# Attention and a sine mixture on one core: angles rounded straight from PSUM, and the exponentials ordered around the sines

## The chip, the cores and the metric

The kernel runs on one core of a Trainium2 chip. The metric is the time of one execution on the device in microseconds; the median of three runs is quoted. Engines are named as the profile names them: PE is TensorE (matrix products, and transposes as products with a unit matrix), DVE is VectorE, ACT is ScalarE, POOL is GpSimd, SP is SyncE, which issues most of the DMA.

## The reference

Two layers follow each other. Attention over 8 batches of 8 heads, 576 positions and head size 64, keeps for each query only the scores within `tau` of that row's largest. The mixture then works on each batch as a 576 x 512 matrix.

```python
scores = scale * q @ k.T                      # per batch and head, 576 x 576
thresh = max(scores, -1, keepdims) - tau
attn = exp(where(scores >= thresh, scores, -1e9) - max)
x = (attn / (sum(attn) + 1e-9)) @ v           # 576 x 512 per batch, heads side by side
theta = x @ w_theta                           # 512 x 512
y = w_tok_r @ (x * cos(theta)) + w_tok_i @ (x * sin(theta))
u = x + y
out = u + maximum(u @ w_ch, 0)
```

## The kernel before

Attention goes over 32 pairs of heads, four to a batch. A pair has 4 units of 128 query rows for each of its two heads, and a ninth step for the last 64 rows of both, so nine steps ("halves"). One half goes through these instructions:

- score: TensorE multiplies q and k into `s_ps`, of which there is one buffer (L278); VectorE copies it out with its sign turned and takes the row minimum as it goes (`sc`, L282).
- softmax: VectorE makes the limit of the row (`nm`, L295), ScalarE the exponentials (`s_sb`, L299), VectorE compares, multiplies and sums in one scalar_tensor_tensor (L300).
- flip: TensorE transposes `s_sb` into `t_ps` (L326, L341), ScalarE copies it out (L331, L333, L344, L348).
- values: twice a pair, 20 matmuls make `o_ps` (L361), and ScalarE copies it to `xT` (L362).
- normalize: once a pair, the reciprocals of the row sums are spread by TensorE (`rb_ps` L377, `rl_ps` L381) and multiplied in by VectorE (L383, L386).

Scores and softmax are issued three halves ahead of the flips. The tiles `t_ps`, `o_ps`, `rb_ps`, `rl_ps`, and `m_ps`, `z_ps`, `y_ps` below share six PSUM buffers, so a matmul that starts a new tile waits until the oldest of the six has been read out.

When the four pairs of a batch are through, the mixture of that batch (`moe`) is woven in between the halves of the next batch. It is a generator that gives TensorE's work out in small groups; `fill()` takes from it as much as falls due. For each of four blocks m of 128 columns it does:

- angle: TensorE makes the angle in two pieces of 288 columns (`m_ps`, L405). Each piece is copied to `th` in units of full turns, by ScalarE for m = 0 and 1 (L444) and by VectorE for m = 2 and 3 (L446). When both pieces are there, VectorE rounds `th` to whole turns by adding and subtracting a large constant, MAGIC (`km`, L453), and subtracts (`th`, L454).
- sines, for two blocks at a time (m = 0 and 1 are the first series, 2 and 3 the second): VectorE makes the absolute value (`z`, L463), ScalarE loads the table of the sine (L467), makes cosine (L471, a sine of a quarter turn less the absolute value) and sine (L472) of both blocks, and loads the table of the exponential again (L476). GpSimd multiplies the four results by x (`z`, L483); in the last batch VectorE does that.
- flips of z: TensorE transposes `z` (L495), ScalarE rounds to a high part (`zh`, L497), VectorE takes the rest (`zl`, L498).
- token: TensorE multiplies with the token weights (`y_ps`, L512), VectorE adds to `xT` (L515). Later follow the products with `w_ch` (L405 again) and L560.

The order within a batch is `a0 a1 s01 a2 a3f0 s23 t0f1 t1f2 t2f3 t3`: a an angle product, s a series of sines, f a flip of z, t a token product. The tiles `th`, `km`, `rb`, `qraw` and `kraw` share four buffers ("t576").

The order of TensorE's instructions is the order in which the code is written (`manual_schedule`). The order on the other engines is made by a scheduler from priorities and a timeline of its own: attention is lifted by `ATTENTION`, the ScalarE instructions of a series by `SINES`. `after(a, b)` asks for a behind b on one engine, without a semaphore. Before the change, nothing says how the exponentials L299 stand to a series, except its lift: one that comes due inside a series takes its own two table loads with it.

Of the kernel before, what the change touches and what calls it, by code (L numbers as in the profile page):

```python
# [12 lines left out]
U32 = mybir.dt.uint32  # L13
AF = mybir.ActivationFunctionType
ALU = mybir.AluOpType
# [24 lines left out]
def tile_attn_moe(  # L40
# [70 lines left out]
    def temp(name, dt=F32):  # L111
        return pool.tile([P, S], dt, tag="t576", name=name, bufs=4)
# [5 lines left out]
        return ins  # L118

    turn = [0]  # L120

    def load_weight(src, n, on_pe=True):

# [168 lines left out]
    def softmax(u, j):  # L292

        nm = u.nm
        nc.vector.tensor_scalar(  # L295
            out=nm[:, 2 + j : 3 + j], in0=nm[:, j : j + 1], scalar1=span, scalar2=None, op0=ALU.add
        )
        e = u.s[:, j]
        nc.scalar.activation(out=e, in_=u.ps[j], func=AF.Exp, bias=nm[:, j : j + 1], scale=-1.0)  # L299
        nc.vector.scalar_tensor_tensor(  # L300
            out=e,
            in0=u.ps[j],
            scalar=nm[:, 2 + j : 3 + j],
            in1=e,
            op0=ALU.is_le,
            op1=ALU.mult,
            accum_out=u.pr.rows[:, 2 * u.i + j : 2 * u.i + j + 1],
        )
# [119 lines left out]
    def moe(b):  # L428
# [7 lines left out]

        def angle(m):
            th = temp("th")
            wm = get_wm(0, m)

            def evict(ps, hs):

                if m < 2:
                    nc.scalar.activation(out=th[:, hs], in_=ps[:, :HS], func=AF.Copy, scale=1.0 / TURN)  # L444
                else:
                    nc.vector.tensor_scalar(  # L446
                        out=th[:, hs], in0=ps[:, :HS], scalar1=1.0 / TURN, scalar2=None, op0=ALU.mult
                    )

            yield from product(wm, xs, evict, m == 0)  # L450

            km = temp("km")
            nc.vector.tensor_scalar(out=km, in0=th, scalar1=MAGIC, scalar2=-MAGIC, op0=ALU.add, op1=ALU.add)  # L453
            nc.vector.tensor_tensor(out=th, in0=th, in1=km, op=ALU.subtract)  # L454
            zs[m, "f"] = th

        def sines(ms):

            todo = []
            for m in ms:  # L460
                th = zs.pop((m, "f"))
                z = pool.tile([P, 2 * S], F32, tag="z", name="z", bufs=3)
                ab = nc.vector.tensor_scalar(  # L463
                    out=z[:, :S].bitcast(U32), in0=th.bitcast(U32), scalar1=0x7FFFFFFF, scalar2=None, op0=ALU.bitwise_and
                )
                todo.append((m, th, z))
            ahead_of = after(nc.scalar.preload_act_table(AF.Sin), ab)  # L467
            with tc.high_priority(offset=SINES):
                for m, th, z in todo:
                    ins = [  # L470
                        nc.scalar.activation(out=z[:, :S], in_=z[:, :S], func=AF.Sin, scale=-TURN_IN, bias=half_pi),  # L471
                        nc.scalar.activation(out=z[:, S:], in_=th, func=AF.Sin, scale=TURN_IN),  # L472
                    ]
                    for x in ins:
                        after(x, ahead_of)
                exp = nc.scalar.preload_act_table(AF.Exp)  # L476
                for x in ins:
                    after(exp, x)
            for m, th, z in todo:
                x = xT[b * NP + m]  # L480
                for i in range(2):
                    zi = z[:, i * S : i * S + S]
                    lo_eng.tensor_tensor(out=zi, in0=zi, in1=x, op=ALU.mult)  # L483
                zs[m] = z
# [215 lines left out]
```

## Time and profile before

| | |
|---|---|
| median of 3 runs | 1151.12 us (1150.61 to 1152.89) |
| span of the profiled execution | 1147.4 us; the page gives no other time of this execution |
| TensorE busy | 1043.9 us, 91% |
| VectorE busy | 869.0 us, 76% |
| ScalarE busy | 750.0 us, 65% |
| GpSimd busy | 375.1 us, 33% |
| granted TensorE clock | 0.98 of full speed in the mean |
| chain that ended last | TensorE 64%, VectorE 15%, ScalarE 13%, issue 4%, DMA 2% |

A row of a timeline begins with the start in us from the span's start and the length in us; a run of equal instructions is one row with "x" and its count. The bracket at its end is how long the engine stood idle before it and what released it. Only the last releaser is named, and what stood ahead of that releaser on its own engine has to be looked up in that engine's timeline.

### The profile page before, as it was taken

The page shows a single profiled execution, that of the slowest core. Times are in us where ns is not written, and L with a number is a line of the kernel's source. Part 1 is how long each engine was busy: PE and PEld are TensorE (multiplying, and loading weights), DVE is VectorE, ACT ScalarE, POOL GpSimd, SP SyncE. Part 2 cuts the span into 40 slices and gives each one's busy share as a digit, 9 for nine tenths or more (in the row PEclk, how much of TensorE's full clock was granted, in tenths as well). Part 3 has the DMA queues.
Part 4 walks back from the last instruction along what each step waited for, and adds up shares of the span by engine and source line. Part 5 has one row for each costly group of instructions (what it writes and reads, how often), then busy time and mean ns, then how long its engine had stood idle before and what let it go on. Part 6 is the DMA issues. An engine that isn't in the chain of part 4 may idle for free.

```text
span 1147.4 us, 21175 instructions
## 1 busy us (share of the span) xinstructions
PE 1043.9 (91%) x7736; PEld 921.5 (80%) x7736; DVE 869.0 (76%) x2139; ACT 750.0 (65%) x1394; POOL 375.1 (33%) x303
## 2 busy tenths in 40 slices
PE   4888888799899998999979998999989999799998
PEld 3566687688779987898869987799878998689898
DVE  7998777987877677876787768776788678787362
ACT  6766869666676566964677666865678656774350
POOL 2203325233342243521443234422435314430210
PEclk9999999999999998999999999999999999999999
DMA  7722223255231052213432142311522133310421
GB/s 252 213 81 84 64 71 97 88 138 148 76 100 53 28 178 74 79 47 103 116 100 63 32 146 76 102 53 34 173 87 72 43 113 104 97 32 1 120 71 60
DMA packets 55176, 105.26 MB, mean 92 GB/s; under 512 B 11936, under 2 KB 20128, under 8 KB 55072
## 3 DMA queue, kind: packets, MB, share of 16 engines
q1 hardware_dynamic: 45856, 70.35, 20.9%
q0 software_dynamic: 9216, 33.56, 10.2%
q8 instruction: 61, 1.00, 0.4%
q14 instruction: 43, 0.35, 0.1%
HBM read 90.24 MB, written 13.63 MB: 91 GB/s over the span
## 4 chain that ended last, share of the span: by engine, by line
PE 64%; DVE 15%; ACT 13%; issue 4%; DMA 2%; POOL 1%; SPq 0%; ACTq 0%; POOLq 0%; DVEq 0%
PE y_ps L512 15%; PE m_ps L405 13%; PE o_ps L361 13%; PE s_ps L278 11%; PE t_ps L326 7%; DVE sc L282 3%; DVE s_sb L300 3%; DVE km L453 3%; ACT s_sb L299 3%; DMA qraw<-in_qT_dram 2%; ACT a L331 2%; PE rb_ps L377 1%; PE z_ps L495 1%; ACT z L471 1%; ACT z L472 1%
## 5 line engine op out<-in xcount | busy, mean ns | idle before, releaser
L300 DVE SCALAR_TENSOR_TENSOR s_sb<-sc,nm,s_sb 128x576 f32<-128x576 f32 x288 | 276.1, 960 | 69.4 <-ACT s_sb L299 65.5
L299 ACT ACTIVATE s_sb<-sc,nm 128x576 f32<-128x576 f32 x288 | 224.1, 778 | 110.8 <-DVE sc L282 109.9
L278 PE MATMUL s_ps<-k,qq 128*128 128x288 f32 (+1 forms) x1344 | 240.2, 307 | 53.8 <-DVE sc L282 39.8
L282 DVE TENSOR_SCALAR_CACHE_REDUCE sc<-s_ps 128x576 f32<-128x576 f32 x288 | 216.7, 753 | 67.2 <-PE s_ps L278 64.3
L278 PEld LDWEIGHTS s_ps<-k,qq 128*128 128x128 f32 x1344 | 193.8, 192 | 81.4 <-DVE sc L282 46.6
L361 PE MATMUL o_ps<-a,v 128*64 128x320 f32 (+1 forms) x1280 | 180.2, 430 | 31.2 <-DVE nm L295 27.7
L331 ACT COPY a<-t_ps 128x512 f32<-128x512 f32 x256 | 148.2, 579 | 58.2 <-PE t_ps L326 56.9
L326 PE MATMUL t_ps<-ident,s_sb 128*128 128x128 f32 x1152 | 175.4, 275 | 1.7 <-DVE zl L498 1.7
L361 PEld LDWEIGHTS o_ps<-a,v 128*64 128x64 f32 x1280 | 92.5, 143 | 97.8 <-ACT s_sb L299 30.4
L512 PE MATMUL y_ps<-wt_h,zh 128*128 128x288 f32 x576 | 165.2, 305 | 6.3 <-DVE zl L498 4.8
L512 PE MATMUL y_ps<-wt_l,zh 128*128 128x288 f32 x576 | 163.0, 301 | 0.0
L109 POOL TENSOR_TENSOR k<-kraw,k 128x576 fp32r<-128x576 f32 x62 | 90.8, 1465 | 202.4 <-ACT k L100 201.0
L228 POOL TENSOR_TENSOR qq<-qraw,qq 64x576 fp32r<-64x576 f32 x62 | 95.1, 1534 | 159.9 <-ACT qq L226 130.4
L326 PEld LDWEIGHTS t_ps<-ident,s_sb 128*128 128x128 f32 x1152 | 142.4, 142 | 3.8 <-DVE zl L498 1.9
L512 PEld LDWEIGHTS y_ps<-wt_h,zh 128*128 128x128 f32 x576 | 108.6, 188 | 8.1 <-DVE zl L498 6.2
L512 PEld LDWEIGHTS y_ps<-wt_l,zh 128*128 128x128 f32 x576 | 108.6, 189 | 0.0
L512 PE MATMUL y_ps<-wt_h,zl 128*128 128x288 f32 x576 | 103.6, 306 | 0.0
L192 POOL DMA_DIRECT2D wm<-wm_dram x64 | 36.4, 570 | 171.0 <-PE m_ps L405 142.6
L405 PE MATMUL m_ps<-xh,wm 128*128 128x288 f32 x512 | 91.5, 305 | 0.3 <-ACT xh L100 0.3
L483 POOL TENSOR_TENSOR z<-z,xT 128x576 f32<-128x576 f32 x56 | 80.0, 1457 | 31.5 <-ACT z L471 31.4
L109 POOL TENSOR_TENSOR ul<-xT,uh 128x576 fp32r<-128x576 f32 x24 | 34.7, 1448 | 169.8 <-DVE uh L104 169.8
L405 PE MATMUL m_ps<-uh,wm 128*128 128x288 f32 x512 | 84.0, 299 | 0.0
(85 smaller groups left out, 1641.9 us busy)
## 6 DMA issues: line engine op xcount, KB each, us to landing
wm<-wm_dram POOLq DMA_DIRECT2D x64, 512.0 KB, 4.0
qraw<-in_qT_dram SPq DMA_DIRECT2D x128, 144.0 KB, 2.9
kraw<-in_kT_dram SPq DMA_DIRECT2D x128, 144.0 KB, 2.9
out_dram<-xT SPq DMA_DIRECT2D x32, 288.0 KB, 2.2
v<-in_vp_dram SPq DMA_DIRECT2D x32, 256.0 KB, 2.7
wraw<-in_w_tok_dram SPq DMA_DIRECT2D x9, 576.0 KB, 5.0
wraw<-in_w_theta_dram SPq DMA_DIRECT2D x4, 512.0 KB, 4.4
wm_dram<-whi SPq DMA_DIRECT2D x8, 256.0 KB, 2.3
```

The source lines that it names most:

```text
L109: eng_lo.tensor_tensor(out=lo, in0=src, in1=hi.bitcast(F32), op=ALU.subtract)
L228: eng.tensor_tensor(out=qq[64:128], in0=raw[64:128], in1=qq[64:128].bitcast(F32), op=ALU.subtract)
L278: nc.tensor.matmul(ps[:, h, d0:d1], st, kk, start=(x == 0), stop=(x == len(todo) - 1))
L282: nc.vector.tensor_scalar(out=sc.rearrange("p (a b) -> p a b", a=2), in0=ps[:, :, :HS], scalar1=-1.0, scalar2=None, op0=ALU.mult, op1=ALU.min,
L299: nc.scalar.activation(out=e, in_=u.ps[j], func=AF.Exp, bias=nm[:, j : j + 1], scale=-1.0)
L300: nc.vector.scalar_tensor_tensor(out=e, in0=u.ps[j], scalar=nm[:, 2 + j : 3 + j], in1=e, op0=ALU.is_le, op1=ALU.mult, accum_out=u.pr.rows[ ...
L326: nc.tensor.transpose(out=tp[:, c * P : (c + 1) * P], in_=u.sf[:, k0 + c * P : k0 + (c + 1) * P], identity=ident)
L331: nc.scalar.copy(out=t.a[:, :, j, q0 : q0 + P], in_=tp.rearrange("p (c q) -> p c q", c=4))
L361: nc.tensor.matmul(o[64 * j : 64 * j + 64, :w], st, mv, start=(c == 0), stop=(c == 4))
L405: nc.tensor.matmul(tiles[h][:, :HS], wm[:, a, c, :], parts[c][bb][:, hs], start=(count[h] == 0), stop=(count[h] == 11))
L483: lo_eng.tensor_tensor(out=zi, in0=zi, in1=x, op=ALU.mult)
L512: nc.tensor.matmul(ps[:, :HS], z, w, start=(n == 0), stop=(n == len(work) - 1))
```

## The change

Four edits, all in the mixture's angles and sines but the last:

- `km` is computed in `evict`, from PSUM, piece by piece: angle times 1/TURN plus MAGIC (two instructions of 128x288 in place of one of 128x576). Its tile is taken at the start of the angle, with `th`.
- the subtraction of MAGIC and of `th` is one scalar_tensor_tensor, (km - MAGIC) - th. Its sign is the other way round, so the sine's scale changes its sign.
- the absolute value is max(-th, th) in a scalar_tensor_tensor, in place of clearing the sign bit.
- the load of the sine table is ordered behind all exponentials issued since the last series; exponentials issued later are ordered behind the load of the exponential table.

In the changed file lines up to 298 move down by one, softmax's exponential is L300 and its L300 becomes L304, the table loads are L473 and L485.

```diff
--- before.py
+++ after.py
@@ -118,6 +118,7 @@
         return ins
 
     turn = [0]
+    table = SimpleNamespace(back=None, exps=[])
 
     def load_weight(src, n, on_pe=True):
 
@@ -296,7 +297,10 @@
             out=nm[:, 2 + j : 3 + j], in0=nm[:, j : j + 1], scalar1=span, scalar2=None, op0=ALU.add
         )
         e = u.s[:, j]
-        nc.scalar.activation(out=e, in_=u.ps[j], func=AF.Exp, bias=nm[:, j : j + 1], scale=-1.0)
+        ins = nc.scalar.activation(out=e, in_=u.ps[j], func=AF.Exp, bias=nm[:, j : j + 1], scale=-1.0)
+        if table.back is not None:
+            after(ins, table.back)
+        table.exps.append(ins)
         nc.vector.scalar_tensor_tensor(
             out=e,
             in0=u.ps[j],
@@ -436,6 +440,7 @@
 
         def angle(m):
             th = temp("th")
+            km = temp("km")
             wm = get_wm(0, m)
 
             def evict(ps, hs):
@@ -446,12 +451,15 @@
                     nc.vector.tensor_scalar(
                         out=th[:, hs], in0=ps[:, :HS], scalar1=1.0 / TURN, scalar2=None, op0=ALU.mult
                     )
+                nc.vector.tensor_scalar(
+                    out=km[:, hs], in0=ps[:, :HS], scalar1=1.0 / TURN, scalar2=MAGIC, op0=ALU.mult, op1=ALU.add
+                )
 
             yield from product(wm, xs, evict, m == 0)
 
-            km = temp("km")
-            nc.vector.tensor_scalar(out=km, in0=th, scalar1=MAGIC, scalar2=-MAGIC, op0=ALU.add, op1=ALU.add)
-            nc.vector.tensor_tensor(out=th, in0=th, in1=km, op=ALU.subtract)
+            nc.vector.scalar_tensor_tensor(
+                out=th, in0=km, scalar=MAGIC, in1=th, op0=ALU.subtract, op1=ALU.subtract
+            )
             zs[m, "f"] = th
 
         def sines(ms):
@@ -460,22 +468,24 @@
             for m in ms:
                 th = zs.pop((m, "f"))
                 z = pool.tile([P, 2 * S], F32, tag="z", name="z", bufs=3)
-                ab = nc.vector.tensor_scalar(
-                    out=z[:, :S].bitcast(U32), in0=th.bitcast(U32), scalar1=0x7FFFFFFF, scalar2=None, op0=ALU.bitwise_and
-                )
+                ab = nc.vector.scalar_tensor_tensor(out=z[:, :S], in0=th, scalar=-1.0, in1=th, op0=ALU.mult, op1=ALU.max)
                 todo.append((m, th, z))
             ahead_of = after(nc.scalar.preload_act_table(AF.Sin), ab)
+            for x in table.exps:
+                after(ahead_of, x)
+            table.exps = []
             with tc.high_priority(offset=SINES):
                 for m, th, z in todo:
                     ins = [
                         nc.scalar.activation(out=z[:, :S], in_=z[:, :S], func=AF.Sin, scale=-TURN_IN, bias=half_pi),
-                        nc.scalar.activation(out=z[:, S:], in_=th, func=AF.Sin, scale=TURN_IN),
+                        nc.scalar.activation(out=z[:, S:], in_=th, func=AF.Sin, scale=-TURN_IN),
                     ]
                     for x in ins:
                         after(x, ahead_of)
                 exp = nc.scalar.preload_act_table(AF.Exp)
                 for x in ins:
                     after(exp, x)
+                table.back = exp
             for m, th, z in todo:
                 x = xT[b * NP + m]
                 for i in range(2):
```

TensorE's instructions stand in the same order in both. On the other engines the scheduler makes another order. The rows below are of the batch whose first series lies at 304 to 310 us in the trace of before; `th_3438` and `th_3514` are the angles of m = 2 and m = 3 before, `th_3444` and `th_3521` the same after.

VectorE at the first series, before: the copies of the third angle's two pieces, its rounding, and what stands behind it.

```order
L282 TENSOR_SCALAR sc_3486,nm_3480<-s_ps_3481 128x576
L446 TENSOR_SCALAR th_3438<-m_ps_3474 128x288
L295 TENSOR_SCALAR nm_3480<-nm_3480,small_74 128x1
L453 TENSOR_SCALAR km_3511<-th_3438 128x576
L282 TENSOR_SCALAR sc_3531,nm_3480<-s_ps_3526 128x576
L454 TENSOR_TENSOR th_3438<-th_3438,km_3511 128x576
L446 TENSOR_SCALAR th_3514<-m_ps_3517 128x288
L295 TENSOR_SCALAR nm_3480<-nm_3480,small_74 128x1
L463 TENSOR_SCALAR z_3659<-th_3438 128x576
L300 SCALAR_TENSOR_TENSOR s_sb_3479,rows9_3393<-sc_3486,nm_3480,s_sb_3479 128x576
```

VectorE at the same place after (L451 is the copy of a piece, L454 the rounding, L460 the subtraction, L471 the maximum, L304 the masked product of softmax).

```order
L451 TENSOR_SCALAR th_3444<-m_ps_3448 128x288
L296 TENSOR_SCALAR nm_3488<-nm_3488,small_74 128x1
L451 TENSOR_SCALAR th_3444<-m_ps_3482 128x288
L283 TENSOR_SCALAR sc_3539,nm_3488<-s_ps_3534 128x576
L454 TENSOR_SCALAR km_3445<-m_ps_3448 128x288
L454 TENSOR_SCALAR km_3445<-m_ps_3482 128x288
L296 TENSOR_SCALAR nm_3488<-nm_3488,small_74 128x1
L451 TENSOR_SCALAR th_3521<-m_ps_3525 128x288
L460 SCALAR_TENSOR_TENSOR th_3444<-km_3445,th_3444 128x576
L454 TENSOR_SCALAR km_3522<-m_ps_3525 128x288
L471 SCALAR_TENSOR_TENSOR z_3667<-th_3444 128x576
L304 SCALAR_TENSOR_TENSOR s_sb_3401,rows9_3400<-sc_3458,nm_3402,s_sb_3401 128x576
```

Both roundings of m = 2 now read `m_ps` and stand one behind the other, ahead of the first piece of m = 3 (`m_ps_3525`). The subtraction comes after that piece, and three masked products follow the maximum; before, a masked product came between these groups.

In TensorE's program `o_ps_3567` (L361) stands before with waits on VectorE and on ScalarE, where VectorE's is for the copy of `m_ps_3517`; after, the same product waits on VectorE for the rounding of `m_ps_3482`.

ScalarE at the first series, before (L467 and L476 are the table loads, L299 the exponentials).

```order
L299 ACTIVATE s_sb_3394<-sc_3451,nm_3395 128x576
L331 COPY a1_3312<-t_ps_3465 128x4x128
L344 COPY a51_3313<-t5_ps_3471 128x128
L467 ACT_TABLE_LOAD
L471 ACTIVATE z_3424<-z_3424,small_74 128x576
L472 ACTIVATE z_3424<-th_3266 128x576
L472 ACTIVATE z_3426<-th_3327 128x576
L471 ACTIVATE z_3426<-z_3426,small_74 128x576
L476 ACT_TABLE_LOAD
L333 COPY a1_3312<-t_ps_3500 128x8x64
L348 COPY a51_3313<-t5_ps_3506 64x64 x2
L299 ACTIVATE s_sb_3479<-sc_3486,nm_3480 128x576
```

ScalarE at the same place after.

```order
L335 COPY a1_3318<-t_ps_3473 128x4x128
L348 COPY a51_3319<-t5_ps_3479 128x128
L473 ACT_TABLE_LOAD
L480 ACTIVATE z_3430<-z_3430,small_74 128x576
L481 ACTIVATE z_3430<-th_3270 128x576
L481 ACTIVATE z_3432<-th_3332 128x576
L337 COPY a1_3318<-t_ps_3509 128x8x64
L480 ACTIVATE z_3432<-z_3432,small_74 128x576
L485 ACT_TABLE_LOAD
L300 ACTIVATE s_sb_3401<-sc_3458,nm_3402 128x576
L300 ACTIVATE s_sb_3487<-sc_3494,nm_3488 128x576
```

The exponential of `sc_3451`, ahead of the series before, is that of `sc_3458` behind it after; the copy `a1` (L333, now L337) has moved in between the sine and the cosine of the second block.

ScalarE at the second series of the same batch, before.

```order
L467 ACT_TABLE_LOAD
L471 ACTIVATE z_3659<-z_3659,small_74 128x576
L472 ACTIVATE z_3659<-th_3438 128x576
L472 ACTIVATE z_3661<-th_3514 128x576
L331 COPY a0_3545<-t_ps_3730 128x4x128
L344 COPY a50_3546<-t5_ps_3736 128x128
L299 ACT_TABLE_LOAD
L299 ACTIVATE s_sb_3712<-sc_3719,nm_3713 128x576
L471 ACT_TABLE_LOAD
L471 ACTIVATE z_3661<-z_3661,small_74 128x576
L476 ACT_TABLE_LOAD
```

ScalarE at that place after.

```order
L473 ACT_TABLE_LOAD
L480 ACTIVATE z_3667<-z_3667,small_74 128x576
L481 ACTIVATE z_3667<-th_3444 128x576
L481 ACTIVATE z_3669<-th_3521 128x576
L335 COPY a0_3554<-t_ps_3738 128x4x128
L348 COPY a50_3555<-t5_ps_3744 128x128
L480 ACTIVATE z_3669<-z_3669,small_74 128x576
L485 ACT_TABLE_LOAD
L300 ACTIVATE s_sb_3720<-sc_3727,nm_3721 128x576
```

The exponential with its Exp load, and the Sin load behind it, are no longer inside the series. Over the whole program ScalarE's table loads go from 47 to 33: the seven at L299 and the seven at L471 are gone.

Of the DMAs, the issue of the first `qraw` on SP moves behind the loads of `v` in each steady batch; on GpSimd the products of `qq` (L228) move by a place or two among the `wm` loads and the products `z`.

## Rows read from the trace of the kernel before

**Rows 1.** Page, part 1: busy time, share of the span, instructions.

```profile
PE 1043.9 (91%) x7736; PEld 921.5 (80%) x7736; DVE 869.0 (76%) x2139; ACT 750.0 (65%) x1394; POOL 375.1 (33%) x303
```

**Rows 2.** Waits: who waited for whom; total us, times, longest us.

```profile
PE o_ps L361 <- DVE nm L295: 27.7, 7, 4.5
...
PE y_ps L512 <- DVE zl L498: 4.8, 6, 0.8
...
PE o_ps L361 <- DVE xT L515: 3.4, 7, 0.5
...
PE s_ps L278 <- DVE rows L366: 3.0, 7, 0.7
```

**Rows 3.** Timeline of TensorE: start, length (us), line, operation, tile, [idle before <- releaser].

```profile
309.15 0.78 PE L405 MATMUL m_ps<-xh,wm 128*128 128x288 f32 x4
314.40 5.55 PE L361 MATMUL o_ps<-a,v 128*64 128x320 f32 x20 [4.47 <-DVE nm L295]
...
321.65 0.60 PE L326 MATMUL t_ps<-ident,s_sb 128*128 128x128 f32 x4
...
323.18 0.69 PE L278 MATMUL s_ps<-k,qq 128*128 128x288 f32 x4
```

**Rows 4.** Timeline of VectorE, the same place.

```profile
307.10 5.44 DVE L453 TENSOR_SCALAR km<-th 128x576 f32<-128x576 f32 x1
312.46 0.74 DVE L282 TENSOR_SCALAR_CACHE_REDUCE sc<-s_ps 128x576 f32<-128x576 f32 x1
...
313.81 0.44 DVE L446 TENSOR_SCALAR th<-m_ps 128x288 f32<-128x288 f32 x1
```

**Rows 5.** Timeline of VectorE, the stretch just before it.

```profile
303.14 0.46 DVE L453 TENSOR_SCALAR km<-th 128x576 f32<-128x576 f32 x1
303.63 0.76 DVE L454 TENSOR_TENSOR th<-th,km 128x576 f32<-128x576 f32 x1
304.31 0.81 DVE L300 SCALAR_TENSOR_TENSOR s_sb<-sc,nm,s_sb 128x576 f32<-128x576 f32 x1
...
305.05 0.46 DVE L463 TENSOR_SCALAR z<-th 128x576 uint32<-128x576 uint32 x1
```

**Rows 6.** Timeline of GpSimd, the same place.

```profile
306.71 5.51 POOL L483 TENSOR_TENSOR z<-z,xT 128x576 f32<-128x576 f32 x4
```

**Rows 7.** Windows: stretch, its length, busy us by engine, PEclk, DMA share, GB/s.

```profile
314.40:320.00 5.60, 5.60 (x21) 2.53 (x22) 2.42 (x6) 1.50 (x3) 0.00 (x0) 0.52 0.19 55
```

**Rows 8.** Chain of waits, two runs of the same shape: start, length, instructions.

```profile
350.48 2.84 PE o_ps L361 x20
...
981.88 4.60 PE o_ps L361 x20
```

**Rows 9.** Timeline of TensorE, a shorter pause.

```profile
287.14 0.79 PE L278 MATMUL s_ps<-k,qq 128*128 128x288 f32 x4 [1.58 <-DVE sc L282]
```

**Rows 10.** Windows, the stretch behind that pause.

```profile
287.20:293.00 5.80, 5.80 (x45) 5.72 (x45) 4.94 (x13) 3.34 (x7) 2.51 (x4) 1.00 0.32 93
```

**Rows 11.** Timeline of ScalarE, the second series of the same batch.

```profile
330.96 1.28 ACT L299 ACT_TABLE_LOAD   x1
...
333.05 1.28 ACT L471 ACT_TABLE_LOAD   x1
```

**Rows 12.** Groups of instructions: busy us, mean ns of one, idle before.

```profile
L300 DVE SCALAR_TENSOR_TENSOR s_sb<-sc,nm,s_sb 128x576 f32<-128x576 f32 x288 | 276.1, 960 | 69.4 <-ACT s_sb L299 65.5
...
L453 DVE TENSOR_SCALAR km<-th 128x576 f32<-128x576 f32 x32 | 45.4, 1420 | 6.9 <-ACT th L444 6.3
...
L446 DVE TENSOR_SCALAR th<-m_ps 128x288 f32<-128x288 f32 x32 | 14.4, 450 | 2.7 <-PE m_ps L405 2.7
...
L299 ACT ACT_TABLE_LOAD x7 | 9.0, 1283 | 0.1
```

**Rows 13.** Timeline of ScalarE, the first series.

```profile
302.96 0.78 ACT L299 ACTIVATE s_sb<-sc,nm 128x576 f32<-128x576 f32 x1 [0.19 <-DVE sc L282]
...
308.33 1.28 ACT L476 ACT_TABLE_LOAD   x1
```

## The prediction, made before the changed kernel ran

> **What bounds the kernel now.** I read the shares of the span first [rows 1]: TensorE is busy 91% of it. With TensorE that full, the time can fall only where TensorE waits or runs slowly, so the second view is what its waits ended on [rows 2]. The largest is 27.7 us in seven waits ahead of the product of attention and values (`o_ps`, L361), the longest 4.5 us. The view names L295 on VectorE as releaser; the timelines show what really stood there. TensorE ends a group of angle products at 309.15 + 0.78 = 309.93 and starts `o_ps` at 314.40 [rows 3]. VectorE meanwhile spends 307.10 to 312.54 in one rounding, `km` L453 [rows 4], which in an undisturbed place takes 0.46 us [rows 5]. GpSimd runs its four products `z` L483 from 306.71 to 312.22 [rows 6]. So the rounding stood still until all four were through, and behind it in VectorE's order stood L446, which empties the PSUM buffer that `o_ps` takes; it came at 313.81 [rows 4].
>
> The wait has a second price. In the stretch behind it the granted clock is 0.52, which is the lower level, 1.2 GHz [rows 7]. The run of 20 `o_ps` matmuls takes 5.55 us in this batch [rows 3] and 4.60 at the sixth such place, against 2.84 for the same run undisturbed [rows 8]. The chain of waits holds all six; they add up to 28.2 us, 11.2 above 6 x 2.84. The first batch's wait is short (27.7 less six of about 4.5 leaves 0.8) and its run is no part of this. A pause of 1.58 us elsewhere [rows 9] is followed by a stretch at 1.00 [rows 10], so short waits cost only themselves.
>
> The third loss lies around the second series of sines of a batch. There ScalarE loads the Exp table at 330.96, does one exponential, and loads the Sin table again at 333.05, inside one series [rows 11]. VectorE's work behind it comes late, and TensorE waits for `zl` L498, for the `xT` update L515 and for the row sums L366: 4.8 + 3.4 + 3.0 = 11.2 us in all [rows 2].
>
> **The change part by part.**
>
> *Rounding from PSUM.* One L453 of 128x576 becomes two of 128x288 that read PSUM. The nearest row is L446, the same engine, shape and source, at 450 ns mean over 32 [rows 12]. So 4 x 2 x 0.45 = 3.6 us a batch, instead of a measured 4 x 1.42 = 5.7 [rows 12], or 4 x 0.46 = 1.8 where nothing disturbs. The gain is not in these sums but in the place: in the new order both roundings of the third angle product (m = 2) stand ahead of the instructions that GpSimd can hold, and `o_ps` waits for the second of them. When VectorE gets there: today it reaches the rounding at 307.10. Up to the same point the new order drops one L300, L453, L454 and L463 (0.81 + 0.46 + 0.76 + 0.46 = 2.49 [rows 5]) and adds two roundings of 0.45 and two scalar_tensor_tensor at 0.81 (2.52), and has one more score copy L282 of 0.74 [rows 4]: 307.9. That copy follows a score which ends about then, so I take 308.2, and 309.1 for the end of both roundings, ahead of TensorE's 309.93. The 27.7 us go, and with them the 11.2 us of low clock. If VectorE were late by one GpSimd product (5.51/4 = 1.38 us [rows 6]), a wait of 0.5 us would be left.
>
> *The subtraction with MAGIC, and the absolute value as a maximum.* Both become scalar_tensor_tensor with two inputs in SBUF. The nearest rows are L300, the same operation and shape, 0.81 clear [rows 5] and 0.96 on the mean [rows 12], and L454, 0.76 clear [rows 5]; below, nothing would make it cheaper than the 0.46 of L463. I take 0.81. For the absolute value that is 0.35 us more than L463, 1.4 us a batch. Clear VectorE work rises from 4 x (0.46 + 0.76 + 0.46) = 6.7 to 4 x (0.90 + 0.81 + 0.81) = 10.1 us a batch; against that the roundings lose the 5.44 - 0.46 = 5.0 us for which one was held. What is now exposed to GpSimd is the subtraction of the third product, issued at about 309.4 with two or three products still to run. Bounds: it slips in when the running product ends (so it is done at 310.3 or 311.6), or it waits for all four, as the rounding did (313.0). Behind it stand the rounding of the fourth product's first half, whose buffer TensorE needs for `rb_ps` at 309.93 + 2.84 = 312.8, then the absolute value, then three L300.
>
> The Trainium skill has a rule that speaks against this part. SBUF — State Buffer, section "Who interferes with whom", says that a VectorE instruction with two SBUF inputs contends with a GpSimd instruction that reads SBUF, that one with a single SBUF input outside the two-port modes does not, and that the one issued first holds the shared ports until it ends. The trace does not bear out that the wait ends with the one running instruction: 5.44 us is four products [rows 4, 6]. By the rule the subtraction is through by 311.6 and `rb_ps` waits for nothing; by the row it is through at 313.0 and `rb_ps` is 0.5 us late.
>
> *Exponentials kept out of the series.* The Sin load waits for the earlier exponentials, and later ones come behind the Exp load. Fourteen table loads go (seven at L299, seven at L471, the built orders hold 47 and 33): 14 x 1.283 = 18.0 us of ScalarE [rows 12], 2.6 us a batch. ScalarE is not the bound, so this is worth only what TensorE waits behind it, inside the 11.2 us above. The price is in the first series: the exponential that ran at 302.96 now comes behind the Exp load that ends at 309.6 today [rows 13], with the next two behind it; with the `a1` copy of 0.6 us now inside the series, the first is done at about 311. The three L300 that use them come behind the absolute value and end at 315.2 in the good case, at 316.4 in the late one. TensorE is 4.47 + 2.71 = 7.2 us earlier there than today: its flips come at 321.65 - 7.2 = 314.5, its next score at 323.18 - 7.2 = 316.0 [rows 3]. That score needs the copy L282 of the one before, which now ends at 316.6 to 317.7: a new wait of 0.6 to 1.7 us, and up to 1.0 more at the next score. With `rb_ps` at 0 to 0.5, and the second series not quite clear, what is left is 0.5 to 4.0 us a batch. I take 2.2, between the good case (about 1.5) and the late one (about 3), as both hand-overs at GpSimd occur in the rows.
>
> **The sum.** Gains 27.7 + 11.2 + 11.2 = 50.1 us. New waits, in seven batches, 7 x 2.2 = 15.4. Net 34.7, so the span falls from 1147.4 to about 1112.7. Of the profiled execution only the span is given; the median of the three runs, 1151.1, is 3.7 above it. With that the forecast is **1116 us**; with 0.5 us left per batch 1104.5, with 4.0 it is 1129.
>
> **The rivals.**
>
> *1. The stall moves and keeps part of its size: about 1140.* For it: the exposed subtraction, three L300 bunched behind one Exp load, and VectorE with 3.4 us more of clear work a batch. TensorE then waits 4.0 us a batch (28 us), half of the low clock stays (5.6) and half of the waits at the second series (5.6): 39 of the 50 come back, 11 are left. Against it: TensorE has angle products, `z` flips and normalizing queued there that need none of these.
>
> *2. No difference: 1149 to 1153.* VectorE's subtraction is held as the rounding was, and TensorE's next wait is as long as that of `o_ps`. Against it: at 309.4 no more than 2.8 us of GpSimd's products are left, and `o_ps` no longer stands behind them.
>
> *3. Slower: about 1159.* VectorE is blocked in both series by its new two-input instructions. This decides from the point where the waits of a steady batch exceed today's 8.2 us (4.5 of wait, 1.87 of low clock, 1.87 at the second series). If the subtraction is issued while all four products are still ahead, it is held for 4.6 us and the low clock costs 1.9 again; if in the second series the exponentials, now behind the Exp load, and a held absolute value make the flips 3.0 us late, that is 9.5 a batch, 1.3 more than now, 8 us over six. The rule of the Trainium skill on two SBUF inputs (the same page and section) points this way. Against it: VectorE has 0.8 us to spare before 309.93, and L300, with two SBUF inputs, has a mean of only 0.96 over 288 executions [rows 12].
>
> **Chances.** Forecast (1104 to 1129) 0.62; rival 1 (1129 to 1148) 0.25; rival 2 0.05; rival 3 0.08. About 0.2%, 2.3 us, is what can be told from no difference. Rival 1 is all on the faster side, so faster is 0.87, same 0.05, slower 0.08. The range takes in the forecast's bounds and the nearer part of rival 1: 1103 to 1142.
>
> **What would show it.** Right: `o_ps` waits for VectorE under 3 us in all, the six runs behind are back at 2.84, no stretch there is at the lower clock, the PSUM roundings take 0.45 beside GpSimd, and 33 table loads are left. New waits then stand at the score (`s_ps` on L282) or the flip (`t_ps` on L300), 1 to 3 us a batch. Wrong: a new wait of 4 us with the low clock behind it; a subtraction or absolute value of 3 us or more while TensorE needs a buffer; exponentials so late that flips wait over 3 us for L300.

## The result, and the profile after

| | before | changed |
|---|---|---|
| median | 1152.0 us (4 runs) | 1123.1 us (4 runs, 1121.0 to 1126.2) |
| profiled execution: span | 1147.4 us | 1121.3 us (its own time 1123.05 us) |
| granted TensorE clock, mean | 0.98 | 0.99 |

The ratio is 0.975, 95% interval 0.973 to 0.977: 2.5% faster. The forecast was 1116 us, the range 1103 to 1142.

The busy times of the page after; they answer to [rows 1].

```profile
PE 1036.1 (92%) x7736; PEld 916.8 (82%) x7736; DVE 860.0 (77%) x2171; ACT 729.5 (65%) x1380; POOL 389.4 (35%) x303
```

The waits of TensorE that are new (who waited for whom; us in total, times, longest). Those of [rows 2] are gone, all four.

```profile
PE t_ps L345 <- DVE zl L508: 7.7, 7, 1.1
...
PE s_ps L279 <- POOL k L109: 6.7, 7, 1.0
...
PE rb_ps L381 <- DVE km L454: 3.9, 6, 0.7
...
PE y_ps L522 <- ACT zh L507: 3.1, 1, 3.1
```

TensorE's timeline at the place of [rows 3], in the same batch. `o_ps` (now L365) follows the angle product without a pause and takes 2.91 us, in place of a wait of 4.47 and a run of 5.55.

```profile
313.58 0.78 PE L409 MATMUL m_ps<-xh,wm 128*128 128x288 f32 x4
314.29 2.91 PE L365 MATMUL o_ps<-a,v 128*64 128x320 f32 x20
317.84 0.66 PE L381 MATMUL rb_ps<-ident,rb 128*128 128x128 f32 x4 [0.64 <-DVE km L454]
...
321.32 0.33 PE L345 MATMUL t_ps<-ident,s_sb 128*128 128x128 f32 x1 [1.11 <-DVE zl L508]
...
325.74 0.53 PE L279 MATMUL s_ps<-k,qq 128*128 128x288 f32 x2 [0.51 <-DVE sc L283]
```

VectorE at that place ([rows 4] before). The two roundings from PSUM are one row of 0.81 us, done at 313.41, ahead of TensorE's 314.29. The instruction that is held now is the subtraction L460, for 3.47 us; it ends at 317.29. Behind it come the rounding whose buffer `rb_ps` takes, and three masked products, the last at 319.85; `zl`, for which the flip waits until 321.32, stands behind those.

```profile
312.60 0.81 DVE L454 TENSOR_SCALAR km<-m_ps 128x288 f32<-128x288 f32 x2
...
313.82 3.47 DVE L460 SCALAR_TENSOR_TENSOR th<-km,th 128x576 f32<-128x576 f32 x1
317.33 0.46 DVE L454 TENSOR_SCALAR km<-m_ps 128x288 f32<-128x288 f32 x1
...
319.85 0.81 DVE L304 SCALAR_TENSOR_TENSOR s_sb<-sc,nm,s_sb 128x576 f32<-128x576 f32 x1
...
320.58 0.68 DVE L508 TENSOR_TENSOR zl<-z_ps,zh 128x512 fp32r<-128x512 f32 x1
```

GpSimd ([rows 6] before): the four products of the first series end at 316.66, and the subtraction, 0.76 us long where it is clear, ends 0.63 us later. In the second series the four take 6.55 us in place of 5.54, and behind them stand `k`, `qq`, `k`.

```profile
311.12 5.54 POOL L493 TENSOR_TENSOR z<-z,xT 128x576 f32<-128x576 f32 x4
...
329.20 6.55 POOL L493 TENSOR_TENSOR z<-z,xT 128x576 f32<-128x576 f32 x4 [3.19 <-ACT z L480]
335.72 1.42 POOL L109 TENSOR_TENSOR k<-kraw,k 128x576 fp32r<-128x576 f32 x1
337.21 1.83 POOL L229 TENSOR_TENSOR qq<-qraw,qq 64x576 fp32r<-64x576 f32 x1
339.12 1.81 POOL L109 TENSOR_TENSOR k<-kraw,k 128x576 fp32r<-128x576 f32 x1
```

For the second of those `k`, which ends at 340.93, TensorE waits at a score:

```profile
340.98 0.67 PE L279 MATMUL s_ps<-k,qq 128*128 128x288 f32 x3 [0.95 <-POOL k L109]
```

The instruction groups that answer to [rows 12] (busy us, mean ns), and the table loads, now 16 and 16 besides the first.

```profile
L460 DVE SCALAR_TENSOR_TENSOR th<-km,th 128x576 f32<-128x576 f32 x32 | 42.0, 1314 | 0.6
...
L454 DVE TENSOR_SCALAR km<-m_ps 128x288 f32<-128x288 f32 x64 | 28.3, 452 | 6.8 <-ACT th L449 6.0
...
L471 DVE SCALAR_TENSOR_TENSOR z<-th 128x576 f32<-128x576 f32 x32 | 24.8, 775 | 0.3
...
L473 ACT ACT_TABLE_LOAD x16 | 20.5, 1283 | 0.3
L485 ACT ACT_TABLE_LOAD x16 | 20.5, 1283 | 0.3
```

The granted clock (the third number from the end of a row) in two stretches of the first series, where it was 0.52 before [rows 7], and in one of the first batch.

```profile
312.00:318.00 6.00, 5.36 (x41) 3.60 (x40) 5.96 (x9) 5.91 (x11) 4.67 (x4) 1.00 0.32 90
318.00:324.00 6.00, 4.89 (x40) 4.65 (x40) 5.85 (x16) 3.66 (x9) 0.59 (x1) 1.00 0.29 89
...
229.30:236.00 6.70, 6.32 (x27) 4.98 (x29) 5.97 (x13) 2.02 (x4) 1.79 (x1) 0.51 0.36 105
```

That last stretch follows a wait of `y_ps` for `zh` in the first batch, 3.07 us (1.46 before), where VectorE prepares weights between the halves; the run of `o_ps` in it takes 3.56 us (2.38 before).

```profile
229.68 0.61 PE L522 MATMUL y_ps<-wt_h,zh 128*128 128x288 f32 x1 [3.07 <-ACT zh L507]
...
233.47 3.56 PE L365 MATMUL o_ps<-a,v 128*64 128x256 f32 x20
```

### The profile page after: what moved, and what is told of

Its sections match the earlier page's. It is cut to its first block, busy times and chain, and to the rows that moved or that the text cites. A ratio compares the mean times of both kernels' runs of the same rounds, so it can differ in the third digit from the quotient of the medians.

```text
span 1121.3 us, 21162 instructions
## 1 busy us (share of the span) xinstructions
PE 1036.1 (92%) x7736; PEld 916.8 (82%) x7736; DVE 860.0 (77%) x2171; ACT 729.5 (65%) x1380; POOL 389.4 (35%) x303
## 4 chain that ended last, share of the span: by engine, by line
PE 66%; DVE 16%; ACT 7%; issue 5%; POOL 2%; DMA 2%; SPq 1%; POOLq 0%; ACTq 0%; DVEq 0%
PE y_ps L522 16%; PE m_ps L409 15%; PE s_ps L279 12%; PE o_ps L365 10%; PE t_ps L330 7%; DVE s_sb L304 4%; DVE sc L283 3%; DVE th L460 2%; PE z_ps L505 1%; PE t_ps L345 1%; POOL k L109 1%; PE rb_ps L381 1%; ACT qraw L226 1%; POOL qq L229 1%; ACT s_sb L300 1%
## 5 line engine op out<-in xcount | busy, mean ns | idle before, releaser
L304 DVE SCALAR_TENSOR_TENSOR s_sb<-sc,nm,s_sb 128x576 f32<-128x576 f32 x288 | 266.0, 927 | 78.4 <-ACT s_sb L300 73.0
L300 ACT ACTIVATE s_sb<-sc,nm 128x576 f32<-128x576 f32 x288 | 223.5, 778 | 97.4 <-DVE sc L283 96.0
L365 PE MATMUL o_ps<-a,v 128*64 128x320 f32 (+1 forms) x1280 | 170.5, 413 | 0.0
L109 POOL TENSOR_TENSOR k<-kraw,k 128x576 fp32r<-128x576 f32 x62 | 93.8, 1514 | 192.6 <-ACT k L100 190.6
L229 POOL TENSOR_TENSOR qq<-qraw,qq 64x576 fp32r<-64x576 f32 x62 | 101.6, 1638 | 111.8 <-ACT qq L227 68.1
L365 PEld LDWEIGHTS o_ps<-a,v 128*64 128x64 f32 x1280 | 86.7, 137 | 62.4 <-issue 6.2
L493 POOL TENSOR_TENSOR z<-z,xT 128x576 f32<-128x576 f32 x56 | 85.3, 1556 | 29.8 <-ACT z L480 29.7
L109 POOL TENSOR_TENSOR ul<-xT,uh 128x576 fp32r<-128x576 f32 x24 | 34.8, 1448 | 155.8 <-DVE uh L104 113.1
```

What stands on the lines that cost most here:

```text
L109: eng_lo.tensor_tensor(out=lo, in0=src, in1=hi.bitcast(F32), op=ALU.subtract)
L229: eng.tensor_tensor(out=qq[64:128], in0=raw[64:128], in1=qq[64:128].bitcast(F32), op=ALU.subtract)
L300: ins = nc.scalar.activation(out=e, in_=u.ps[j], func=AF.Exp, bias=nm[:, j : j + 1], scale=-1.0)
L304: nc.vector.scalar_tensor_tensor(out=e, in0=u.ps[j], scalar=nm[:, 2 + j : 3 + j], in1=e, op0=ALU.is_le, op1=ALU.mult, accum_out=u.pr.rows[ ...
L365: nc.tensor.matmul(o[64 * j : 64 * j + 64, :w], st, mv, start=(c == 0), stop=(c == 4))
```

## The experiments

All times are medians, with the ratio to the kernel before and its interval; 0.9748 (0.9729 to 0.9768) is the change. It ran once more beside e9 to e11: 1123.0 us, 0.9748 (0.9729 to 0.9767).

> The changed kernel once more, beside e9 to e11 on the same chip, to compare them with it directly: 1121 to 1126.

**The parts of the change.** e1 has only the order of the exponentials:

```diff
+        if table.back is not None:
+            after(ins, table.back)
+        table.exps.append(ins)
...
+            for x in table.exps:
+                after(ahead_of, x)
```

> The kernel before with nothing but the order of the exponentials around the series of sines (33 table loads in place of 47). Theory A (the gain of the change is the place of the roundings, ahead of what GpSimd's products can hold): the rounding of the third angle product is still one 128x576 instruction from SBUF beside the four products, so o_ps still waits for VectorE, 4 us or more in each of six batches (over 24 us in all), with the lower clock (1.2 GHz) behind it; only the waits around the second series go, at most 11 us. Time 1138 to 1150. Rival B (the gain is ScalarE's: 18 us fewer table loads and exponentials that no longer split a series): time about as with the whole change, 1120 to 1128, and o_ps waits under 5 us.

It took 1157.3 us, 1.005 (1.003 to 1.007): slower than before. The rounding L457 is still held (4.38 us in the steady batches), and `o_ps` waits for the copy L450 behind it. So theory A held in its mechanism and rival B fell, but `o_ps` waited less than A's 24 us and the time lies above A's upper end of 1150: the gain that I expected was eaten by new waits, of `y_ps` for `zh` (7.4 us) among them, and by the first batch. The last `o_ps` run ahead of the first steady series starts 7.5 us later than before (300.65 against 293.15); from there to the same run of the last batch both take the same time, 768.6 and 768.8 us. The wait ahead of `o_ps` is 3.3 us in each of the six steady batches; in four of them the run behind it takes 4.6 to 5.6 us, in two it takes 2.91, so a wait of that length did not always have the low clock right behind it.

```profile
PE o_ps L365 <- DVE th L450: 19.6, 6, 3.3
...
PE y_ps L520 <- ACT zh L505: 7.4, 4, 3.1
```

```profile
L457 DVE TENSOR_SCALAR km<-th 128x576 f32<-128x576 f32 x32 | 39.3, 1228 | 6.4 <-ACT th L448 6.3
```

e2 has only the roundings from PSUM and the one subtraction (lines against the change, cut at "..."):

```diff
-                ab = nc.vector.scalar_tensor_tensor(out=z[:, :S], in0=th, scalar=-1.0, in1=th, op0=ALU.mult, op1=ALU.max)
+                ab = nc.vector.tensor_scalar(
+                    out=z[:, :S].bitcast(U32), in0=th.bitcast(U32), scalar1=0x7FFFFFFF, scalar2=None, op0=ALU.bitwise_and
+                )
...
-            for x in table.exps:
-                after(ahead_of, x)
...
-                table.back = exp
```

> The change without its order of the exponentials and with the absolute value as before (sign bit cleared): only the roundings from PSUM and the one subtraction. 47 table loads, as before. Theory A: o_ps waits for VectorE under 3 us in all and the runs of 20 behind it take 2.84; the waits around the second series stay, about 11 us; time 1123 to 1136. Rival B: the table loads are what counts, so the time stays at 1143 or more.

1137.2 us, 0.987 (0.984 to 0.989). No wait of `o_ps` for a rounding is left; the theory's range was missed by 1 us. In this build `o_ps` takes a buffer that ScalarE's copy of `a1` frees. The waits that are left are at `z_ps` and the score. Theory A had the 11 us at the second series stay; they did not. In this order the exponential with its table loads falls into the first series of each batch, not the second, where TensorE waits 1.1 us for `xT`. In that split first series GpSimd's fourth product comes 1.81 us after the third; the subtraction is held for 1.98 us, not 3.47, and ends 0.6 us after the third product (317.71).

```profile
PE z_ps L500 <- ACT a L332: 7.4, 7, 1.1
...
PE o_ps L362 <- ACT a L332: 1.8, 7, 0.3
```

```profile
313.54 4.17 POOL L488 TENSOR_TENSOR z<-z,xT 128x576 f32<-128x576 f32 x3
319.53 1.55 POOL L488 TENSOR_TENSOR z<-z,xT 128x576 f32<-128x576 f32 x1 [1.81 <-ACT z L476]
```

```profile
316.36 1.98 DVE L457 SCALAR_TENSOR_TENSOR th<-km,th 128x576 f32<-128x576 f32 x1
```

e9 is e2 with the maximum, that is the change without its order:

> The whole change without its order of the exponentials (47 table loads as before; the maximum stays). o_ps draws the buffer of ScalarE's a1 copy here, as in e2, and not one that a rounding frees. Theory F (what counts is which instruction frees the buffer that o_ps draws, and what stands ahead of it): no wait of o_ps on VectorE, time about that of e2, 1132 to 1140. Rival B' (with the roundings in place the order of the exponentials is worth nothing): 1121 to 1127.

1128.0 us, 0.979 (0.977 to 0.981), between the two expectations: 5 us above the change that ran beside it, and 9 below e2. All four runs of e9 (1124.9 to 1129.6) lie above all four of the change (1120.7 to 1123.6), so beside the new roundings and the maximum the order is worth about 5 us (the exponential falls into the first series here, as in e2), and rival B' fell; theory F had no wait of `o_ps` on VectorE right, but not the time. The wait at `z_ps` is that of e2, 7.4 us.

```profile
PE z_ps L498 <- ACT a L332: 7.4, 7, 1.1
```

e3 is the change with the absolute value as before (first two lines of e2's diff):

> The whole change, but the absolute value clears the sign bit as before, with one input in SBUF, in place of the maximum with two. Theory A: the absolute value is not on the path where it stands (it comes behind the end of GpSimd's products), so the time is that of the change within 0.3% (1120 to 1127); one of it takes about 0.46 us where it is clear, 0.3 us less than the maximum, and the three masked products behind the first series end 0.3 us earlier. Rival C (the second SBUF input of the maximum is what leaves new waits): 3 to 8 us faster than the change. Rival D (clearing the sign bit is held by GpSimd and the maximum is not): slower by 3 us or more, with single executions of L471 over 1.5 us.

1148.6 us, 0.998 (0.997 to 1.000): 25 us slower than the change, for one instruction that is itself 0.19 us shorter in the mean (L471 587 ns against 775); in the steady first series it takes 0.45 us, and its longest execution anywhere is 1.43. Theory A and rivals C and D all fell: D's time came, by another way. The subtraction is held as in the change (3.46 us), but here `o_ps` waits until after it; in five of the six steady batches the run behind that wait takes 4.4 to 4.6 us, in the one shown 2.91. The second `o_ps` run of each batch has a new wait too, 8.4 us in all, for a copy on ScalarE.

```profile
PE o_ps L365 <- DVE km L454: 23.4, 7, 3.6
...
PE o_ps L365 <- ACT a L335: 8.4, 7, 2.3
```

```profile
315.29 2.91 PE L365 MATMUL o_ps<-a,v 128*64 128x320 f32 x20 [3.56 <-DVE km L454]
```

```profile
311.20 3.46 DVE L460 SCALAR_TENSOR_TENSOR th<-km,th 128x576 f32<-128x576 f32 x1
314.69 0.46 DVE L454 TENSOR_SCALAR km<-m_ps 128x288 f32<-128x288 f32 x1
315.06 0.45 DVE L471 TENSOR_SCALAR z<-th 128x576 uint32<-128x576 uint32 x1
```

The built programs show what changed, and the wait in e3 agrees. In the change `o_ps` takes the PSUM buffer that the second rounding of m = 2 frees, ahead of the subtraction. In e3 it takes the one of the first piece of m = 3, whose rounding (314.69) stands behind it. So the buffer that a new tile takes is not always the oldest of the six, as the section on the kernel has it: with the same order on TensorE it was another one in e3. I take it that the scheduler gives the buffers out by its own timeline, in which the shorter instruction made another one the free one; no run shows how it chooses. e5 tests the draw: everything as in e3, but the rounding goes ahead of the subtraction (`subtract` issues it).

```diff
-                nc.vector.tensor_scalar(
+                r = nc.vector.tensor_scalar(
                     out=km[:, hs], in0=ps[:, :HS], scalar1=1.0 / TURN, scalar2=MAGIC, op0=ALU.mult, op1=ALU.add
                 )
+                if pending:
+                    after(subtract(*pending.pop()), r)
...
+            if m == 2:
+                pending.append((th, km))
+            else:
+                subtract(th, km)
```

> The kernel of e3 (the change, but the absolute value clears the sign bit) with one thing moved: the subtraction of the third angle product comes behind the rounding of the fourth one's first half. Theory F (the 25 us that e3 lost lie in the PSUM buffer that o_ps drew: that of the fourth product's first half, whose rounding stood behind the held subtraction; the change's maximum only led the scheduler to another draw): o_ps waits for VectorE under 3 us in all, the subtraction may still be held for 3 us, and the time is 1115 to 1127. Rival G (clearing the sign bit is itself what costs): the time stays above 1140.

1136.2 us, 0.986 (0.983 to 0.989). `o_ps` waits no more for a rounding, but 13.4 us for ScalarE's `a1`, whose buffer it now takes, and the low clock behind it is gone. So 12 of e3's 25 us came back and rival G fell; but theory F's 1127 was missed by 9 us, and the other 13 are not explained by that wait of `o_ps` on VectorE. As `o_ps` took a third buffer here, e5 does not put the draw alone back to that of the change. Of the 13.8 us by which its span (1135.1) is longer than the change's, 4.3 lie ahead of the steady batches, 1.4 in the mean in each of the six, and 1.1 behind them.

```profile
PE o_ps L365 <- ACT a L337: 13.4, 8, 1.9
```

**What is left in the change.** e6 makes e5's move in the change itself:

> The whole change with the subtraction of the third angle product behind the rounding of the fourth one's first half. Theory F: rb_ps no longer waits for L454 (3.9 us in the change); the flips still wait for what stands behind the held subtraction; 1116 to 1123. Rival H (the waits are given by the end of GpSimd's products, and what is won at rb_ps comes back at the flip): within 0.2% of the change, 1121 to 1126.

1125.8 us, 0.978 (0.976 to 0.980): not told apart from the change. `rb_ps` waits for nothing, and as rival H had it the wait came back, at `z_ps`:

```profile
PE z_ps L515 <- DVE km L461: 4.8, 7, 0.7
...
PE z_ps L515 <- DVE xT L387: 2.5, 7, 0.4
```

e7 orders the subtraction behind the masked products instead:

```diff
+            if m == 2:
+                for x in table.masks:
+                    after(sub, x)
```

> The whole change with the subtraction of the third angle product ordered behind the masked products of the halves begun by then, so two of the three masked products and no long-held instruction stand ahead of it. Theory F: the flips no longer wait for zl behind three masked products (7.7 us in the change) and rb_ps waits for nothing; 1112 to 1120. Rival H (a masked product has two inputs in SBUF as well and is held until GpSimd's four products are through): the first masked product takes over 1.5 us in each steady batch and the time stays within 0.3% of the change.

1123.2 us, 0.976 (0.973 to 0.979): the same as the change. `rb_ps` waits for nothing, but the waits at the flips fell only from 7.7 to 6.9 us (4.3 + 2.6), so theory F's 1120 was missed. Rival H came in both parts: the first masked product, with two inputs in SBUF, now takes 1.95 to 1.97 us in each of the six steady batches, in place of 0.81. What is held is whatever two-input instruction stands there, not the subtraction as such.

```profile
PE t_ps L346 <- DVE zl L513: 4.3, 7, 0.6
...
PE t_ps L331 <- DVE km L455: 2.6, 7, 0.4
```

```profile
315.47 1.97 DVE L304 SCALAR_TENSOR_TENSOR s_sb<-sc,nm,s_sb 128x576 f32<-128x576 f32 x1 [1.43 <-ACT s_sb L300]
```

e8 does away with the second SBUF input of the subtraction. With it go the copies of the angle, also those that ScalarE made for m = 0 and 1, and the maximum of m = 2 is moved, so its time is that of all of these together:

```diff
-            km = temp("km")
+            km = temp("km", I32)
...
                 nc.vector.tensor_scalar(
-                    out=km[:, hs], in0=ps[:, :HS], scalar1=1.0 / TURN, scalar2=MAGIC, op0=ALU.mult, op1=ALU.add
+                    out=km[:, hs], in0=ps[:, :HS], scalar1=1.0 / TURN, scalar2=None, op0=ALU.mult
                 )
+                ins = nc.vector.scalar_tensor_tensor(
+                    out=th[:, hs], in0=ps[:, :HS], scalar=-1.0 / TURN, in1=km[:, hs], op0=ALU.mult, op1=ALU.add
+                )
...
+                if m == 2:
+                    after(ab, table.half)
```

> The change with another subtraction: the rounding writes whole turns as 32-bit integers from PSUM, and one scalar_tensor_tensor takes them from the angle in PSUM, piece by piece; no copy of the angle, and no subtraction with two inputs in SBUF. The maximum of m = 2 comes behind the first piece of m = 3. Theory F: no such subtraction beside GpSimd takes over 0.6 us (one input in SBUF), VectorE has 0.8 us less work for each of m = 2 and 3, and the time is 1108 to 1120. Rival I (both reads hold the PSUM buffer longer, and the maximum is held in the place of the subtraction): o_ps or z_ps wait for L452 by 1 us or more a batch, 1122 to 1135.

1119.6 us, 0.973 (0.970 to 0.975). The subtraction takes 453 ns in the mean and is never held (at most 458); the maximum now is, at 1076 ns in the mean. The time is theory F's; of rival I the held maximum came, but `m_ps` waits for L452 only 0.5 us a batch. It is the fastest median of all, but its interval overlaps that of the change, and they did not run side by side.

```profile
L468 DVE SCALAR_TENSOR_TENSOR z<-th 128x576 f32<-128x576 f32 x32 | 34.4, 1076 | 0.3
...
L452 DVE SCALAR_TENSOR_TENSOR th<-m_ps,km 128x288 f32<-128x288 f32 x64 | 28.3, 453 | 0.4
```

```profile
PE m_ps L410 <- DVE th L452: 3.4, 7, 0.5
```

**The products taken off GpSimd.** e4 is the kernel before with its four products per series on VectorE:

```diff
-        lo_eng = nc.vector if last else nc.gpsimd
+        lo_eng = nc.vector
```

> The kernel before with the four products z per series on VectorE in all batches in place of GpSimd: nothing of GpSimd's runs beside the rounding. Theory A (the rounding stood still for GpSimd's products): L453 has a mean near 0.46 us and no execution of 5 us, though VectorE has 8 products of 0.75 us, 6 us a batch, more to do. The time is not foreseen, as this work comes onto VectorE (1130 to 1170). Rival E (the rounding was held by something else, such as a write of ScalarE or the wait of a semaphore): L453 still has executions of over 4 us in the same place.

A single run: 1130.0 us, 21 below the kernel before beside it (1151.3). The rounding, with its place in the source unchanged, has a mean of 459 ns and no execution over 1 us; rival E fell. So it was GpSimd's products that held it. Taking them away gave most of the gain, in spite of 6 us more of VectorE's work a batch; but `o_ps` also takes another buffer here (its waits are for ScalarE's copies, 3.0 and 2.4 us), so the 21 us are not shown to come from the hold alone.

```profile
L483 DVE TENSOR_TENSOR z<-z,xT 128x576 f32<-128x576 f32 x64 | 47.2, 748 | 10.3 <-ACT z L471 10.3
...
L453 DVE TENSOR_SCALAR km<-th 128x576 f32<-128x576 f32 x32 | 14.7, 459 | 6.4 <-ACT th L444 6.3
```

e10 makes the same edit in the change, e11 in e8:

> The whole change with the four products z per series on VectorE in place of GpSimd in all batches. Theory A: the subtraction of the third product is never held (L460 near 0.76 us in every execution, against 3.47), and the waits of rb_ps on it (3.9 us) are gone; but VectorE has 6 us a batch more, so the time lies between 1112 and 1128. Rival H (waits at the flip and the score come from the bunch of masked products, not from GpSimd): waits of t_ps and s_ps stay at 2 us a batch or more and the time is that of the change or above it, 1121 to 1132.

1120.8 us, 0.973 (0.972 to 0.975): 2 us below the change, within the intervals. The subtraction is no longer held by the products (859 ns in the mean; once a batch it still waits beside `qq`), `rb_ps` waits for nothing, and new waits are at the flip for ScalarE, 0.7 us a batch, so rival H's 2 us fell.

```profile
L460 DVE SCALAR_TENSOR_TENSOR th<-km,th 128x576 f32<-128x576 f32 x32 | 27.5, 859 | 0.6
```

```profile
PE t_ps L345 <- ACT a L335: 4.7, 7, 0.7
```

> e8 (rounding to integers, subtraction from PSUM) with the four products z per series on VectorE in all batches, so that nothing of VectorE's angles runs beside GpSimd's products. Theory A: the maximum falls from 1.08 us in the mean to 0.75, and as there is less work than in e10, the time is 1108 to 1118. Rival J (VectorE is then full enough to be late itself): 1120 to 1130, with waits of s_ps on sc and of z_ps on zl.

1127.9 us, 0.979 (0.976 to 0.981): the time of rival J, and VectorE is late, but with the `xT` update, 13.3 us in all, and not where J had it. Theory A's 0.75 us for the maximum was missed as well: the mean is 1024 ns, as once a batch it takes 2.0 us beside `qq`.

```profile
PE y_ps L521 <- DVE xT L524: 13.3, 7, 1.9
```

## Why the prediction was right, and where it was off

*The wait of `o_ps` and the low clock.* Right: 27.7 us and six runs of 4.3 to 5.6 us became no wait and runs of 2.9. The reasons hold: GpSimd's products held the rounding (e4), and PSUM roundings beside GpSimd take 452 ns in the mean, 458 at most. But the step leans on something that I read from the built program and did not weigh: which buffer `o_ps` takes. With another (e3) almost all of the gain is gone, though the rounding is just as quick.

*The second series.* The 11.2 us of waits there are gone in the change; a new one, for GpSimd, has come (below). That the order of the exponentials is worth them is not shown: e1 was slower than before, and beside the roundings alone the order cost time (e2 1137, e3 1149). e9 against the change gives 5 us, but in e2 and e9 it is the first series that is split, and the waits at the second are mostly gone without the order. The parts do not add: order 1157, roundings 1137, roundings with the maximum 1128, roundings with the order 1149, all 1123.

*The held subtraction.* The late case came: the hand working had it end at 313.0, 0.8 us behind the products; it ended 0.6 us behind them, and `rb_ps` was 0.64 late (0.5 expected). Behind that the prediction had 0.6 to 1.7 us at one score and up to 1.0 at the next; measured were 1.11 at a flip, for `zl` behind the three masked products, and 0.51 at a score. So one of the signs of being wrong did appear, a subtraction of over 3 us while TensorE needs a buffer; it cost 0.64 us and not 4, because `o_ps` no longer stands behind what is held.

*Mis-sized: what is left per batch, 2.2 us.* It is 0.64 + 1.11 + 0.51 + 0.95 = 3.2. The first three make 2.26. The last, TensorE waiting for `k` L109 on GpSimd, was in no term: ScalarE's second `qq` cast came behind the series, so GpSimd's `qq`, which before ran at 326 ahead of the products, now stood between the two `k`; it and the second `k` took 1.8 us each, the first `k` 1.42. Seven such waits make 6.7 us; the span of 1112.7 was missed by 8.6. The first batch adds a longer wait of `y_ps` (3.07 against 1.46) with a low clock behind it, of which the forecast had nothing: the `o_ps` run ahead of the first steady series starts 4.4 us later than before (297.56 against 293.15), of which the repeat e12 shows 3.0. From there to the same run of the last batch the change takes 738.5 us, 30.4 less than before, where the forecast has about 34.5 for the six steady batches. So of the 8.6 us about half lie ahead of the steady batches, and the waits for `k` are in part offset by smaller terms.

The step from span to time was off the other way: the forecast added 3.7 us, but in the profiled run after the two differ by 1.75 (1123.05 against 1121.3), and in the runs before on record by about as much. So about 2 of the 3.7 came from a profiled run before that was quicker than the median; by luck they hid 2 us of the miss.

*The rivals.* 1, 2 and 3 did not come as whole cases. The number of table loads came as said: 33. On the clock the prediction had one pause of 1.58 us without a low stretch behind it. Waits of 3.1 us (first batch) and 3.3 us (e1, four of six) had one; behind others of 3.3 and 3.6 us (e1, e3) the run of `o_ps` was at full clock.

*Two inputs in SBUF.* The subtraction waited through the rest of one product and two whole ones. Readers of PSUM were not held in any kernel here, and neither was e8's subtraction, with one input in SBUF. The rounding before had one input in SBUF and was held for 5.44 us. In the second series GpSimd gave way too: 6.55 us for four products. The rule of the Trainium skill that the prediction weighed (SBUF — State Buffer, "Who interferes with whom") is borne out in which instructions are held, not in that the wait ends with the one instruction that was issued first. For the rounding before, the rule holds only if that ran in one of the two-port modes; no trace here names the mode.

Open: why the hold spans all products that follow each other without a pause in the first series (it ended at the pause in e2 and e9, at the last product in the others) and sometimes one in the second, and why e2 and e9, alike in the draw of `o_ps`, lie 9 us apart. Untested is the PSUM reading apart from the draw: no run keeps the old rounding beside GpSimd and gives `o_ps` a buffer that VectorE does not free.

## What to carry to other kernels

Look for an instruction far above its own clear duration, see what runs beside it on the other engines (here GpSimd), and then ask what stands behind it in that engine's order and who takes the buffer it frees. Where a scheduler gives out buffers, read from the built program which one the waiting instruction takes: an edit of 0.2 us elsewhere can change that. Here two kernels that differ by such an edit lie 25 us apart, and 12 of these came back when one rounding was moved. Parts of such a change can't be priced alone.

## What had not been expected of the hardware

A VectorE instruction that reads one 128x576 tile from SBUF and takes 0.46 us stood for 5.44 us through four GpSimd products of 1.4 us each; in the change the two-input subtraction stood for 3.5 us through the last two, in e3 likewise. A scalar_tensor_tensor of 128x576 with two SBUF inputs, clear of GpSimd, takes 0.75 to 0.76 us, not 0.81 (L471, 775 ns in the mean). Writing a product as 32-bit integers from PSUM costs no more than writing it as floats: L449 in e8 takes 454 ns in the mean, L454 in the change 452.
